# Idle matmuls in the boot, and one decay level to a phase instead of two, in an fp32 linear-attention and feed-forward kernel

## The chip, the core and the metric

The kernel runs on one core of one Trainium2 chip. The metric is device time in microseconds (us), the median of three runs. A core has a matmul engine (TensorE, called PE in the profile, with its weight loads apart as PEld), two elementwise engines (VectorE, called DVE, and ScalarE, called ACT), GpSimd (POOL), and queues that start transfers (SP is one). Each works through its own instructions in order and waits for the others by semaphores. Matmul results land in PSUM, everything else lies in SBUF.

## What is computed

```python
# first: linear attention with a decaying state, 4 batches, 8 heads, 768 tokens, 48 channels
for t in range(S):
    kt, vt, rt, wt = (k[:, :, t], v[:, :, t], r[:, :, t], w[:, :, t])
    cur = np.einsum('bhd,bhe->bhde', u[None] * kt, vt)
    y[:, :, t] = np.einsum('bhd,bhde->bhe', rt, state + cur)
    state = wt[:, :, :, None] * state + np.einsum('bhd,bhe->bhde', kt, vt)
# then, with x = y as (3072 tokens, 384 channels): w_in is (384, 2048), w_out is (2048, 384)
h = x @ w_in
g = h - np.tanh(h)
out = g @ w_out
```

All of it is fp32. The kernel cuts the 768 tokens of a batch in two, which makes eight blocks of 384 tokens. Within a block, chunks of 64 tokens are worked out by matmuls: the scores between a token and the earlier ones of its chunk are found level by level (spans of m = 1, 2, 4, 8, 16, 32). At each level the keys (`kq`) and receptances (`rp`) are multiplied by the decays of their half spans ("decay"), after the level's matmuls ("gram") have read them, and the part of the scores that belongs to the level is kept.

## The kernel before

The first block's attention is a stage of its own, the boot. After that, the feed-forward part of one block (16 steps f of 128 hidden columns: three matmuls into `hp`, elementwise work, and three steps later three matmuls into `acc`) runs with the attention of the next block in its gaps. The score buffers, the gram and the decay:

```python
    def scratch(ps):
        return ps.tile([P, 2, BANK], F32, name="att", tag="att")     # two PSUM banks
...
        def gram(self, ps, lhs, rhs, p0, n, m, width):               # 12 small matmuls for each of n pairs
            ps_t = scratch(ps)
...
                            nc.tensor.matmul(dst, lhsT=lhs[rows, t0:t0 + L], rhs=src,
                                             start=True, stop=True)
            return used
...
        def decay(self, m, p0, n, which=("kq", "rp")):
...
                ins = nc.vector.tensor_tensor(out=part, in0=part, in1=by, op=ALU.mult)
            return ins

        def level(self, ps, m, p0, n, put_off=None):
            if m == L // 2:
                copies = self.last_level(ps, p0, n)
                if put_off is None:
                    copies()
                else:
                    put_off.append(copies)
                return self.decay(m, p0, n)
            gr = self.gram(ps, self.tiles["kq"], self.tiles["rp"], p0, n, m, L // 2)
            ins = self.decay(m, p0, n)
            self.keep(gr, m, p0, n)
            return ins
```

Two levels in one phase need a second copy of `kq` and `rp`, one before and one after the first level's decay. The half that the decay changes is written there by VectorE, the other half is copied by ScalarE:

```python
        def decay_apart(self, m, name):
...
            nc.vector.tensor_tensor(out=dst[:, :, half, :], in0=src[:, :, half, :], in1=by, op=ALU.mult)

        def copy_half(self, m, name):
...
            nc.scalar.copy(out=dst[:, :, half, :], in_=src[:, :, half, :])

        def two_levels(self, ps, m):
            for i, level in enumerate((m, 2 * m)):
                gr = self.gram(ps, self.pairs["kq"][i], self.pairs["rp"][i], 0, NPAIR, level, L // 2)
                self.keep(gr, level, 0, NPAIR)
...
            self.decay(2 * m, 0, NPAIR)
```

The plan tells at which step f which phase of the next block's attention is put. Block 0 (i == 0) has one level to a phase, the others two:

```python
        names = ("level 1", 2, 4, 8, 16, 32, "turn", "update", "result 1")
        if i == 0:
            steps = (0, 2, 4, 5, 6, 7, 9, 10, 12)
...
        else:
            names = ("level 1", (2, 4), (8, 16), 32, "turn", "update", "result 1")
            steps = (2, 5, 8, 9, 10, 11, 13)
            before = {0: ("totals 1",), 1: ("totals 2", "kq"), 2: ("rp",), 3: (("by", 2, "kq"),),
                      4: (("by", 2, "rp"),), 6: (("by", 8, "kq"), ("by", 8, "rp"))}
            front = {4: (("copy", 2, "kq"),), 5: (("copy", 2, "rp"),), 7: (("copy", 8, "kq"), ("copy", 8, "rp"))}
```

The boot works in two halves of the head pairs, so that one half's gram stands beside the other's decay. The last level's copies (`last`) are put off behind the transposes (`turn`):

```python
        for m in (2, 4, 8, 16, 32):
            for p0 in HALVES:
                if (m, p0) != (2, h1):
                    ins = blk.level(ps, m, p0, UP, last)
                if p0 == h2 or m == 32:
                    blk.totals(m, p0, UP)
...
        for p0 in HALVES:
            blk.turn(ps, p0)
        for copies in last:
            copies()
        later.mix(0, NPAIR, ("kmix",))
        for p0 in HALVES:
            blk.update(ps, p0)
...
    with tc.tile_pool(name="ps_boot", bufs=4, space=PSUM) as ps_boot:
        xT = blocks[0].begin()
        boot(ps_boot, blocks[0], blocks[1])
```

Of the kernel before, what the change touches and what calls it, by code (L numbers as in the profile page):

```python
# [37 lines left out]
F32 = mybir.dt.float32  # L38
# [46 lines left out]
def kernel(  # L85
# [26 lines left out]
    u_sb = const.tile([P, NPAIR], F32, name="u_sb", tag="u_sb")  # L112
    nc.scalar.dma_start(out=u_sb, in_=uT)

    warm = const.tile([P, 1], F32, name="warm", tag="warm")
    nc.scalar.activation(out=warm, in_=shift[:, 0:1], func=AF.Copy)

# [65 lines left out]
    class Block:  # L183


        def __init__(self, b, q):
            self.b, self.q = b, q
            self.cols = slice(q * NB, (q + 1) * NB)
            self.tiles = {}
            self.tots = {}  # L190
            self.ks = {}
            self.pairs = {}

        def load(self, name, src, p0, n):
            if name not in self.tiles:
# [82 lines left out]
# [7 lines that stand above are left out]
                return self.decay(m, p0, n)  # L285
            gr = self.gram(ps, self.tiles["kq"], self.tiles["rp"], p0, n, m, L // 2)
            ins = self.decay(m, p0, n)
            self.keep(gr, m, p0, n)
            return ins

        def keep(self, gr, m, p0, n):
            nb = L // (2 * m)
            if 2 * m % 32 == 0:

                for par in range(2):
                    for b in range(nb):
                        s0, t0 = 64 * par + 2 * m * b, 2 * m * b + m
                        dst = A[s0:s0 + m, :, p0:p0 + n].rearrange("s h p c t -> s h (p c) t")
                        src = gr[s0:s0 + m].rearrange("s h (n b m) -> s h n b m", b=nb, m=m)
                        nc.scalar.copy(out=dst[:, :, :, t0:t0 + m], in_=src[:, :, :, b, :])  # L300
                return
            for h in range(2):
                dst = A[:, h, p0:p0 + n].rearrange("s p c (b two m) -> s (p c) b two m",
                                                   two=2, m=m)[:, :, :, 1, :]
                src = gr[:, h].rearrange("s (n b m) -> s n b m", b=nb, m=m)
                mask = masks[m].bitcast(U8).unsqueeze(1).to_broadcast([P, n * NCP, nb, m])
                nc.vector.copy_predicated(out=dst, mask=mask, data=src)  # L307


        def decay_apart(self, m, name):  # L310

            if name not in self.pairs:
                self.pairs[name] = [self.tiles[name], conv.tile([P, NPAIR * NB], F32, name=name + "_2",
                                                               tag="raw")]
            src, dst = self.pairs[name]
            tot, half = self.tots[m, 0], 0 if name == "kq" else 1
            t2 = tot.rearrange("d (n two) -> d n two", two=2)
            src, dst = (t.rearrange("d (n two m) -> d n two m", two=2, m=m) for t in (src, dst))
            by = t2[:, :, 1 - half].unsqueeze(2).to_broadcast([P, NPAIR * NB // (2 * m), m])
            nc.vector.tensor_tensor(out=dst[:, :, half, :], in0=src[:, :, half, :], in1=by, op=ALU.mult)  # L320

        def copy_half(self, m, name):
            half = 1 if name == "kq" else 0
            src, dst = (t.rearrange("d (n two m) -> d n two m", two=2, m=m) for t in self.pairs[name])
            nc.scalar.copy(out=dst[:, :, half, :], in_=src[:, :, half, :])

        def two_levels(self, ps, m):
            for i, level in enumerate((m, 2 * m)):
                gr = self.gram(ps, self.pairs["kq"][i], self.pairs["rp"][i], 0, NPAIR, level, L // 2)
                self.keep(gr, level, 0, NPAIR)  # L330
            for name, (src, dst) in self.pairs.items():
                self.tiles[name] = dst
                self.pairs[name] = [dst, src]
            self.decay(2 * m, 0, NPAIR)

        def last_level(self, ps, p0, n):

# [139 lines left out]
        def phase(self, ps, name):  # L477
            if name == "level 1":
                for p0 in HALVES:
                    self.level_1(ps, p0)()  # L480
            elif name == "turn":
                for p0 in HALVES:
                    self.turn(ps, p0)
            elif name == "update":
                for p0 in HALVES:
                    self.update(ps, p0)
            elif name in ((2, 4), (8, 16)):
                self.two_levels(ps, name[0])
            elif name == "result 1":
                self.parts = self.result_1(ps, list(range(NPAIR)))  # L490
            elif name == "result 2":
                self.result_2(*self.parts)
                self.fill_holes([nc.sync])
            else:
                self.level(ps, name, 0, NPAIR)


        def prepare(self, name):
# [5 lines left out]
            elif name == "totals 1":  # L504
                for m in (1, 2):
                    self.totals(m, 0, NPAIR)
            elif name == "totals 2":
                for m in (4, 8, 16, 32):
                    self.totals(m, 0, NPAIR)
            elif name in ("kq", "rp"):  # L510
                self.decay(1, 0, NPAIR, (name,))
            else:
                what, m, which = name
                (self.copy_half if what == "copy" else self.decay_apart)(m, which)


    def first(xT, f, ps):
# [49 lines left out]
    def plan(i):  # L567

        names = ("level 1", 2, 4, 8, 16, 32, "turn", "update", "result 1")
        if i == 0:  # L570

            steps = (0, 2, 4, 5, 6, 7, 9, 10, 12)
            before, front, urgent = {}, {}, (4, 5, 6)
            converted = (3, 4, 5, 5, 7, 9, 9, 10, 11, 13)
            loads = {f: "weights" for f in (0, 1, 2, 3, 4, 6, 7, 8, 9, 10)}
            loads.update({5: "v", 11: "rmix", 12: "kmix", 13: "wt", 14: "kq", 15: "rp"})
        else:
            names = ("level 1", (2, 4), (8, 16), 32, "turn", "update", "result 1")
            steps = (2, 5, 8, 9, 10, 11, 13)
            before = {0: ("totals 1",), 1: ("totals 2", "kq"), 2: ("rp",), 3: (("by", 2, "kq"),),  # L580
                      4: (("by", 2, "rp"),), 6: (("by", 8, "kq"), ("by", 8, "rp"))}
            front = {4: (("copy", 2, "kq"),), 5: (("copy", 2, "rp"),), 7: (("copy", 8, "kq"), ("copy", 8, "rp"))}
            converted, urgent = (), ()
            loads = {2: "v", 5: "rmix", 7: "kmix", 9: "wt", 11: "kq", 14: "rp"}
        return dict(zip(steps, names)), before, front, converted, loads, urgent

    blocks = [Block(b, q) for b in range(B) for q in range(NQ)]
    ctx.enter_context(tc.manual_schedule(engines={PE, SP, DVE, ACT}))
# [12 lines left out]
        tc.add_manual_dep(dma.ins, ins.ins.name, mybir.DependencyInfo(  # L601
            mybir.DependencyClass.Sync, mybir.DependencyReason.DATA))

    def boot(ps, blk, later):

        h1, h2 = HALVES
        for p0 in HALVES:
            for name, src in (("kq", kT), ("rp", rT), ("wt", wT)):
                blk.load(name, src, p0, UP)
# [5 lines left out]
            more_weights(nc.sync)  # L615
        blk.mix(h1, UP, copy=nc.vector.tensor_copy)
        masked = blk.level_1(ps, h1)
        blk.decay(1, h1, UP)
        blk.totals(1, h1, UP)
        blk.mix(h2, UP, copy=nc.scalar.copy)  # L620
        masked()
        blk.level(ps, 2, h1, UP)
        masked = blk.level_1(ps, h2)
        blk.decay(1, h2, UP)
        blk.totals(1, h2, UP)
        for m in (2, 4, 8, 16):
# [5 lines left out]
        for m in (2, 4, 8, 16, 32):  # L632
            for p0 in HALVES:
                if (m, p0) != (2, h1):
                    ins = blk.level(ps, m, p0, UP, last)
                if p0 == h2 or m == 32:
                    blk.totals(m, p0, UP)
            if m in background:
# [34 lines left out]
            converted()  # L673
            later.prepare(name)

    with tc.tile_pool(name="ps_boot", bufs=4, space=PSUM) as ps_boot:
        xT = blocks[0].begin()
        boot(ps_boot, blocks[0], blocks[1])
    ps_d = ctx.enter_context(tc.tile_pool(name="ps_d", bufs=1, space=PSUM))
    ps_a = ctx.enter_context(tc.tile_pool(name="ps_a", bufs=2, space=PSUM))  # L680
    waiting, rest, extra = [], [], []
# [11 lines left out]
    for i, blk in enumerate(blocks):  # L693
# [2 lines left out]
        after = blocks[i + 2] if i + 2 < len(blocks) else None  # L696
        if later:
            xT = later.begin()
        phases, before, front, converted, loads, urgent = plan(i)
        second = Second(blk.b * S + blk.q * NB, ps_d)  # L700
        for f in range(NF):
            if later:
                for name in front.get(f, ()):
                    later.prepare(name)
            g, next_rest, made = first(here, f, ps_d)
            waiting.append((second, f, g))
            if f not in urgent:
# [1 line left out]
            if later:  # L709
                for name in before.get(f, ()):  # L710
                    later.prepare(name)
                if f in phases:
                    later.phase(ps_a, phases[f])
            if after and f >= NF - 2:
                after.prepare("kmix" if f == NF - 2 else "rmix")
            if f in urgent:

                finish(rest, extra)
# [69 lines left out]
```

## Time and profile before

| what | value |
|---|---|
| device time, three runs | 678.99, 681.27, 680.66 us; median 680.66 |
| span of the profiled run (678.99 us) | 677.2 us, mean granted TensorE clock 0.977 |
| VectorE busy, share of the span | 546.6 us, 81% |
| ScalarE busy, share of the span | 508.3 us, 75% |
| acc and hp matmuls (L558, L520) | 768 records each, 280.1 and 274.3 us busy |
| grams of the levels 2 to 16 (L243, 48x32) | 3072 records, 56.6 us busy |
| half copies of two-level phases (L325, ScalarE) | 24, 10.4 us (rp) and 10.3 us (kq) busy |
| decays apart (L320, VectorE) | 24, 11.4 us (rp) and 11.4 us (kq) busy |

How to read it: the page of the profile gives each engine's busy time and the chain of work that ended last, followed back from the end. A line of a group names the source line (L243), the engine, the operation, the tiles as out<-in, shape and count (x192). A number in brackets with an arrow, such as [0.82 <-issue], is idle time of that engine just before and what ended it; "issue" means that the engine waited for nothing that the profile shows. In order of time, the first number is the start and the second the length, in us. A line by stages has the stretch, its length, then busy time and count of TensorE matmuls, of weight loads, VectorE, ScalarE and GpSimd, then granted TensorE clock, busy share of the transfer engines and GB/s. Matmuls overlap and their ends are modelled, so that starts are the better measure of pace.

### The profile page before, as it was taken

The page shows a single profiled execution, that of the slowest core. Times are in us where ns is not written, and L with a number is a line of the kernel's source. Part 1 is how long each engine was busy: PE and PEld are TensorE (multiplying, and loading weights), DVE is VectorE, ACT ScalarE, POOL GpSimd, SP SyncE. Part 2 cuts the span into 40 slices and gives each one's busy share as a digit, 9 for nine tenths or more (in the row PEclk, how much of TensorE's full clock was granted, in tenths as well). Part 3 has the DMA queues.
Part 4 walks back from the last instruction along what each step waited for, and adds up shares of the span by engine and source line. Part 5 has one row for each costly group of instructions (what it writes and reads, how often), then busy time and mean ns, then how long its engine had stood idle before and what let it go on. Part 6 is the DMA issues. An engine that isn't in the chain of part 4 may idle for free.

```text
span 677.2 us, 20000 instructions
## 1 busy us (share of the span) xinstructions
PE 648.8 (96%) x8480; PEld 414.6 (61%) x8480; DVE 546.6 (81%) x1101; ACT 508.3 (75%) x992; POOL 4.9 (1%) x19
## 2 busy tenths in 40 slices
PE   5879999999999999999999999999999999999998
PEld 4745556666666656666665656656666666665554
DVE  7779999997769968699887976779867998756764
ACT  4779898876767767687868857678676868778785
POOL 2000000000000000000000000000000000000000
PEclk9969999998999989999999988999999999999999
DMA  8656343431303113221311221113211210000000
GB/s 316 231 181 207 130 142 107 150 106 48 92 13 110 56 49 95 57 71 49 95 48 56 79 89 48 48 57 100 67 51 51 84 40 2 2 11 36 0 0 36
DMA packets 30842, 54.38 MB, mean 80 GB/s; under 512 B 2336, under 2 KB 28704, under 8 KB 30752
## 3 DMA queue, kind: packets, MB, share of 16 engines
q1 hardware_dynamic: 30336, 52.80, 24.2%
q8 instruction: 67, 1.10, 0.7%
q10 hardware_dynamic: 352, 0.25, 0.1%
q14 instruction: 23, 0.19, 0.1%
q0 software_dynamic: 64, 0.05, 0.0%
HBM read 47.19 MB, written 4.72 MB: 77 GB/s over the span
## 4 chain that ended last, share of the span: by engine, by line
PE 87%; DVE 5%; ACT 3%; issue 2%; DMA 1%; PEld 0%; PEldq 0%; SPq 0%; DVEq 0%
PE acc L558 36%; PE hp L520 36%; PE att L243 8%; PE att L437 2%; PE att L419 2%; PE att L373 2%; PE att L391 1%; PE att L350 1%; DVE rp L275 1%; DVE w_sb L175 1%; DMA wt<-in_wT 1%; DVE hs L537 1%; DVE kq L275 1%; DVE scores L307 1%; ACT scores L361 1%
## 5 line engine op out<-in xcount | busy, mean ns | idle before, releaser
L558 PE MATMUL acc<-w_sb,gT 128*128 128x384 f32 x768 | 280.1, 503 | 0.8
L520 PE MATMUL hp<-xT,w_sb 128*128 128x384 f32 x768 | 274.3, 494 | 4.8 <-ACT xT L465 2.1
L520 PEld LDWEIGHTS hp<-xT,w_sb 128*128 128x128 f32 x768 | 146.9, 193 | 110.5 <-issue 6.1
L558 PEld LDWEIGHTS acc<-w_sb,gT 128*128 128x128 f32 x768 | 144.7, 194 | 94.9 <-issue 6.4
L527 ACT ACTIVATE h<-hp 128x384 f32<-128x384 f32 x128 | 62.7, 490 | 116.6 <-PE hp L520 115.6
L542 DVE TENSOR_TENSOR th<-h,th 128x384 f32<-128x384 f32 x128 | 71.0, 555 | 43.9 <-ACT th L531 43.9
L537 DVE SCALAR_TENSOR_TENSOR hs<-h,s 128x384 f32<-128x384 f32 x128 | 70.8, 553 | 22.7 <-ACT s L528 22.7
L545 DVE COPY_PREDICATED gT<-big,th 128x384 f32<-128x384 int32 x128 | 76.3, 596 | 12.4
L529 ACT ACTIVATE qa<-s,shift 128x384 f32<-128x384 f32 x128 | 78.8, 615 | 4.2
L537 DVE SCALAR_TENSOR_TENSOR gT<-qb,hs 128x384 f32<-128x384 f32 x128 | 71.4, 558 | 10.1
L532 ACT ACTIVATE big<-s,shift 128x384 f32<-128x384 f32 x128 | 76.8, 600 | 0.0
L530 ACT ACTIVATE qb<-s,shift 128x384 f32<-128x384 f32 x128 | 76.7, 600 | 0.0
L537 DVE SCALAR_TENSOR_TENSOR hs<-qa,hs 128x384 f32<-128x384 f32 x128 | 70.6, 552 | 0.0
L528 ACT ACTIVATE s<-h 128x384 f32<-128x384 f32 x128 | 67.0, 523 | 4.0
L531 ACT ACTIVATE th<-h 128x384 f32<-128x384 f32 x128 | 64.9, 507 | 0.0
L243 PEld LDWEIGHTS att<-rp,kq 48*64 48x64 f32 x3072 | 53.4, 146 | 18.3 <-issue 11.1
L243 PE MATMUL att<-rp,kq 48*64 48x32 f32 x3072 | 56.6, 229 | 8.0 <-issue 6.0
L275 DVE TENSOR_TENSOR kq<-kq,tot 128x768 f32<-128x768 f32 (+1 forms) x33 | 27.4, 830 | 15.1 <-PE att L350 7.9
L402 DVE SCALAR_TENSOR_TENSOR states<-states,tot,att 128x48 f32<-128x48 f32 x176 | 31.5, 258 | 8.7 <-PE att L391 8.7
L307 DVE COPY_PREDICATED scores<-mask_all,att 128x384 f32<-128x384 uint8 (+1 forms) x54 | 31.4, 663 | 2.3 <-PE att L243 1.7
L275 DVE TENSOR_TENSOR rp<-rp,tot 128x768 f32<-128x768 f32 (+1 forms) x33 | 27.3, 828 | 0.0
L243 PE MATMUL att<-rmix,kmix 48*64 48x64 f32 x768 | 14.5, 232 | 6.7 <-ACT rmix L223 6.7
(58 smaller groups left out, 379.4 us busy)
## 6 DMA issues: line engine op xcount, KB each, us to landing
raw<-in_weights SPq DMA_DIRECT2D x16, 768.0 KB, 4.7
rmix<-in_rT SPq DMA_DIRECT2D x7, 768.0 KB, 4.7
kmix<-in_kT SPq DMA_DIRECT2D x7, 768.0 KB, 4.6
wt<-in_wT SPq DMA_DIRECT2D x7, 768.0 KB, 4.6
kq<-in_kT SPq DMA_DIRECT2D x7, 768.0 KB, 5.4
rp<-in_rT SPq DMA_DIRECT2D x7, 768.0 KB, 4.7
v_sb<-in_v SPq DMA_DIRECT2D x8, 576.0 KB, 4.6
out_y<-o SPq DMA_DIRECT2D x23, 192.0 KB, 1.9
```

Source lines behind the costliest of these rows:

```text
L243: nc.tensor.matmul(dst, lhsT=lhs[rows, t0:t0 + L], rhs=src, start=True, stop=True)
L275: ins = nc.vector.tensor_tensor(out=part, in0=part, in1=by, op=ALU.mult)
L520: nc.tensor.matmul(hp, lhsT=w_in_sb[:, f, kc, :], rhs=xT[:, kc, :], start=(kc == KC - 1), stop=(kc == 0))
L528: nc.scalar.activation(out=s, in_=h, func=AF.Square)
L529: nc.scalar.activation(out=qa, in_=s, func=AF.Square, bias=shift[:, 0:1])
L530: nc.scalar.activation(out=qb, in_=s, func=AF.Square, bias=shift[:, 1:2])
L531: nc.scalar.activation(out=th, in_=h, func=AF.Tanh)
L532: nc.scalar.activation(out=big, in_=s, func=AF.Relu, bias=shift[:, 2:3])
L537: return lambda: nc.vector.scalar_tensor_tensor(out=out, in0=in0, scalar=scalar, in1=in1, op0=op0, op1=ALU.mult)
L542: lambda: nc.vector.tensor_tensor(out=th, in0=h, in1=th, op=ALU.subtract),
L545: lambda: nc.vector.copy_predicated(out=g, mask=big.bitcast(I32), data=th)], made
L558: nc.tensor.matmul(acc, lhsT=g[:, j * P:(j + 1) * P], rhs=w_out_sb[:, f, :], start=(f == 0), stop=(f == NF - 1))
```

## The change

The change has two parts.

In the boot, TensorE gets 16 matmuls whose results nobody reads: 128x128 by 128x384 in fp32, on a tile of ones, into a PSUM bank of their own. They are meant for TensorE's waits, to keep the engine busy there. Four stand at the start and one behind each half level. The bank they need is taken from the boot's score buffers, three of two banks each instead of four.

In blocks 1 to 6, levels 2, 4, 8 and 16 get a phase each, as in block 0, instead of two for each pair of levels. The second tiles, the decays that write there and the half copies go; the ordinary decay in place is used for all levels. The multiplications of `kmix` and `rmix` by u move from the last two steps of a block to the first two of the next, and the other preparations move later by two steps.

```diff
+    idle_in = const.tile([P, NB], F32, name="idle_in", tag="idle_in")
+    nc.vector.memset(idle_in, 1.0)
     warm = const.tile([P, 1], F32, name="warm", tag="warm")
...
-        def decay_apart(self, m, name):
...
-        def copy_half(self, m, name):
...
-        def two_levels(self, ps, m):
...
         else:
-            names = ("level 1", (2, 4), (8, 16), 32, "turn", "update", "result 1")
-            steps = (2, 5, 8, 9, 10, 11, 13)
-            before = {0: ("totals 1",), 1: ("totals 2", "kq"), 2: ("rp",), 3: (("by", 2, "kq"),),
-                      4: (("by", 2, "rp"),), 6: (("by", 8, "kq"), ("by", 8, "rp"))}
-            front = {4: (("copy", 2, "kq"),), 5: (("copy", 2, "rp"),), 7: (("copy", 8, "kq"), ("copy", 8, "rp"))}
-            converted, urgent = (), ()
+            steps = (4, 5, 6, 7, 8, 9, 10, 11, 13)
+            before = {0: ("kmix",), 1: ("rmix",), 2: ("totals 1",), 3: ("totals 2", "kq"), 4: ("rp",)}
+            behind, converted, urgent = {}, (), ()
...
-    def boot(ps, blk, later):
+    def boot(ps, ps_idle, blk, later):
 
         h1, h2 = HALVES
+        spare = ps_idle.tile([P, NB], F32, name="spare", tag="spare")
+
+        def keep_busy(n):
+
+            for _ in range(n):
+                nc.tensor.matmul(spare, lhsT=idle_in[:, 0:P], rhs=idle_in, start=True, stop=True)
+
+        keep_busy(4)
...
         masked = blk.level_1(ps, h1)
+        keep_busy(1)
...
         blk.level(ps, 2, h1, UP)
+        keep_busy(1)
         masked = blk.level_1(ps, h2)
+        keep_busy(1)
...
                 if (m, p0) != (2, h1):
                     ins = blk.level(ps, m, p0, UP, last)
+                    keep_busy(1)
...
-    with tc.tile_pool(name="ps_boot", bufs=4, space=PSUM) as ps_boot:
+    with tc.tile_pool(name="ps_boot", bufs=3, space=PSUM) as ps_boot, \
+            tc.tile_pool(name="ps_idle", bufs=1, space=PSUM) as ps_idle:
         xT = blocks[0].begin()
-        boot(ps_boot, blocks[0], blocks[1])
+        boot(ps_boot, ps_idle, blocks[0], blocks[1])
...
-            if after and f >= NF - 2:
-                after.prepare("kmix" if f == NF - 2 else "rmix")
```

## The prediction

> **What bounds the kernel now.** I read the page's busy row and chain first, then TensorE's instructions in order of time, then what TensorE waited for, stage by stage, then VectorE's order of time in one block and in the boot.
>
> ```profile
> PE 648.8 (96%) x8480; PEld 414.6 (61%) x8480; DVE 546.6 (81%) x1101; ACT 508.3 (75%) x992; POOL 4.9 (1%) x19
> ...
> PE 87%; DVE 5%; ACT 3%; issue 2%; DMA 1%; PEld 0%; PEldq 0%; SPq 0%; DVEq 0%
> ```
>
> TensorE sets the time, and of its 677.2 us 28.4 are idle. What PE's busy time hides is its clock. The output copies (L563) close every block and mark its length: they start at 135.61, 217.55, 298.67, 376.43, 460.14, 541.15 and 618.89 us. The periods are 81.94, 81.12, 77.76, 83.71, 81.01 and 77.74. Two of six are alike to 0.02 us; the other four are longer by 4.2, 3.4, 5.95 and 3.25, **16.8 us in all**. In the order of time, a two-level phase in an undisturbed block (first two lines) and one in a long block:
>
> ```profile
> 323.64 3.00 PE L243 MATMUL att<-rp,kq 48*64 48x32 f32 x192
> 326.57 2.20 PE L558 MATMUL acc<-w_sb,gT 128*128 128x384 f32 x6
> ...
> 145.85 2.76 PE L243 MATMUL att<-rp,kq 48*64 48x32 f32 x174
> 149.43 0.74 PE L243 MATMUL att<-rp,kq 48*64 48x32 f32 x18 [0.82 <-issue]
> 150.11 4.21 PE L558 MATMUL acc<-w_sb,gT 128*128 128x384 f32 x6
> 154.10 2.99 PE L520 MATMUL hp<-xT,w_sb 128*128 128x384 f32 x6
> ```
>
> A phase is 192 matmul records (every fp32 matmul leaves two, each with its weight load). In the second TensorE stops for 0.8 us in mid-phase, with "issue" as the only cause, and the dense matmuls after it take twice as long. The stages around it:
>
> ```profile
> 143.80:149.10 5.30, 4.81 (x181) 3.60 (x180) 5.09 (x9) 5.21 (x10) 0.00 (x0) 1.00 0.26 64
> 149.10:155.90 6.80, 6.47 (x27) 3.80 (x27) 5.92 (x11) 0.00 (x0) 0.00 (x0) 0.50 0.19 70
> 155.90:159.30 3.40, 3.40 (x12) 2.01 (x11) 2.02 (x3) 2.10 (x5) 0.00 (x0) 1.00 0.00 0
> ```
>
> The third number from the end is the granted clock: 0.50 for 6.8 us. Over the blocks, what TensorE waited for shows the same event five times, and little else:
>
> ```profile
> PE att L243 <- issue: 5.6, 5, 1.4
> PE hp L520 <- DVE w_sb L175: 1.6, 4, 0.6
> ```
>
> All five lie in the twelve two-level phases (stops of 0.82, 1.38, 1.21, 0.93, 1.27 us); about thirty single bursts of the same density but half the length show none. Each time a 16 KB packet of the instruction queue starts 1.0 to 1.7 us into the phase (at 147.22 in the case shown), TensorE runs dry shortly after and goes on 2.2 to 2.9 us after the packet's start.
>
> **The boot** (0 to 42.90, the first hp) is the other stretch with a wrong clock:
>
> ```profile
> 15.48 1.51 PE L243 MATMUL att<-rp,kq 48*64 48x32 f32 x48 [0.33 <-DVE rp L275]
> 17.52 6.02 PE L243 MATMUL att<-rp,kq 48*64 48x32 f32 x187 [0.53 <-DVE rp L275]
> ...
> 42.90 4.05 PE L520 MATMUL hp<-xT,w_sb 128*128 128x384 f32 x6 [2.07 <-ACT xT L465]
> ```
>
> 48 records in 1.51 us are 31 ns each; in the blocks 192 take 3.00, 15.6 ns. So the boot's levels run at half clock, although the page prints 9 there (the trace's clock records begin only at 29.6 us). But VectorE is as full there: in 12 to 24.3 us it is busy 11.42 of 12.30 us.
>
> **What the Trainium skill says.** "TensorE: Matmul & The Clock Gate", Part 1 (The HAM clock gate): the clock is halved by default, a busy window of about 3.4 us releases it, an idle one takes it back. The trace agrees: cold spells of 3.4 and 6.8 us, and full rate 3.8 us after the first hp. Part 4 (PE-mode transpose) of that page says transposes don't count as busy; the first clock record (1.00 at 29.6 us) follows 2.8 us of fp32 transposes, so here they seem to. "Runtime: NRT & Kernel Launch", Instruction fetch mechanics: instructions come in blocks of 256 and crossing is "mostly hidden". A two-level phase has 384 TensorE instructions and must cross one; the five stops show it is not always hidden. "PSUM — Partial Sum Buffer", Specifications: eight banks of 512 fp32 values. A score buffer here is two, so four fill PSUM and the idle bank costs the fourth; no trace line bears on that.
>
> **The change part by part.**
>
> 1. *Phases split (blocks 1 to 6).* Same matmuls, same decays on VectorE (two for each level either way; out of place or in place both about 0.95 us). ScalarE loses 24 half copies of 0.86 us, 20.7 us, but no TensorE wait in an undisturbed block names it: worth nothing directly. Each phase is now 96 matmul records, 192 instructions. Block 0 already runs so: its level bursts last 1.53 us start to start (53.77 to 55.30) against 2.93/2 = 1.465, and the dense group before and the one after each cost about 0.1 more than 1.935. Two more bursts in a block: 2 x (0.065 + 0.2) = 0.53, **+3.2 us** in six blocks.
>
> 2. *The stops.* After a fetch starts, TensorE has work for at least 1.0 us (mostly 1.2 to 1.65) at burst rate. A single level lasts 1.5, so only a fetch that falls on its first few tenths can bite. Block 0 has four such bursts without a stop and without a cold spell. Most of the 16.8 us goes. I keep 1.5 back for a few stops of 0.6 us: **-15.3 us**.
>
> 3. *Does a new wait appear?* A level now needs the decay of the level before one step earlier. A step on TensorE is 1.94 (hp) + 1.53 + 1.94 (acc) + 0.1 = 5.5 us. VectorE: five products 2.7 (302.61 to 306.22 less one 0.86 decay, start to start), decays 1.73, masked copies 1.7 (m = 2) or 0.93: 6.1, 5.4, 5.4. Laid out from the end of one hp, with the gram at 5.6 to 7.1: previous copies done by 5.1, products to 7.8, decays to 9.55; the next gram wants them at 11.1. Slack 1.5 us, though one step is over budget by 0.6. Block 0 waited for a decay once, 0.23 us, with converts on top. **0**. The u products move from steps 14 and 15 to steps 0 and 1, where VectorE has 3.6 us of work in 3.87: **0**.
>
> 4. *Idle matmuls.* 4 + 3 + 9 = 16, each two records of 0.323 us warm: 0.645, 10.3 us in all (twice that cold). The first four start behind the memset at about 1.5 us and, cold, end at 1.5 + 8 x 0.65 = 6.7; the first gram started at 5.92. They are over 3.4 us of solid work, so I expect the clock up before they end: delay 0.3. Then a half level is 0.75 (24 matmuls warm) + 0.645 + 0.2 of switching = 1.6 us on TensorE, against VectorE's 1.55 (0.47 + 0.47 for decays, 0.53 to 0.62 for copies, totals between) and today's 1.5. So levels hardly get faster. What goes is VectorE's waits near the end (0.93 at 24.46, some 0.6 at the last level): -1.5, and half the transposes' 2.8 us: -1.4.
>
> 5. *Three buffers.* The last level's two stay occupied until its put-off copies, which stand behind both transposes' copies on ScalarE. The second transposes and the first update wait for one buffer: one copy, 0.8, plus 0.6 of handing over: **+1.4**. After that nothing is kept busy; TensorE idles, 24 state updates on VectorE (30.28 to 34.57) and ScalarE copies set the pace, and the clock falls as today. The 4.05 us first hp stays.
> Sum for the boot: 0.3 - 1.5 - 1.4 + 1.4 = **-1.2 us**.
>
> Total: 3.2 - 15.3 - 1.2 = -13.3 us against the profiled run, 678.99: 665.7. The median before is 680.66, and the undisturbed level the blocks fall to is common to all runs, so a run with more stops gains more; the boot's guess has an edge downwards as well (an issue stop of 2.25 us at 33 us shifts by 64 instructions). I say **665.0 us**.
>
> **Rivals.**
> *A: the cold boot stays cold.* If four idle matmuls don't release the clock, each half level is 1.5 + 1.3 = 2.8 us, 9 x 1.25 = 11 us lost: about 676. For it: the levels alone never warmed it. Against: five to six microseconds of dense matmuls, while the first hp (42.90) reached full rate in 3.8. One in twelve.
> *B: the decay chain becomes the wait.* If VectorE lags by 1 us more than laid out, every level waits about 1 us: 24 x 1 = 24 us, and 689. For it: VectorE is over budget in one step of each block. Against: block 0, with more work, waited 0.23. One in thirty.
> *C: stops have nothing to do with phase length.* Then stops and cold spells return in other bursts and only the boot counts: about 680. Against: five of twelve long phases, none of the short. One in ten.
> *D: no stop at all and a fully warm boot tail* (another 2 us at the first hp): about 660.
>
> **Range and chances.** 2% faster is below 667.05. Main line 662 to 668 by the boot's and the remaining stops' uncertainty; A and C carry the upper end. 80%: 659.5 to 671.5. Faster 0.73, same 0.25, slower 0.02.
>
> **What would show it.** Periods between output copies of 78.0 to 78.6 in blocks 1 to 6; no 0.50 clock after 50 us; "att <- issue" under 2 us; boot grams at 15 to 16 ns a record and the first hp at 41 to 43. Wrong if TensorE waits for "DVE rp" or "kq" in the blocks by more than 3 us, if half clock reappears in the blocks, or if the first hp comes after 45.

## The result, and the profile after

The changed kernel takes 670.13 us (median of four runs, 669.34 to 673.36), the kernel before 680.96 us beside it (678.99 to 681.42). The ratio is 0.9855, with a 95% interval of 0.9817 to 0.9893: 1.45% faster, 10.8 us. The range of the prediction holds it, but the time lies 5.1 us above the 665.0 named, and "faster by over 2%", to which 0.73 was given, did not come about; a change of under 2%, given 0.25, did.

The span of the profiled run went from 677.2 to 668.7 us, by 8.5. Cut at the first `hp` and at the first output copy of each block, it splits so:

| stretch | before | after | difference |
|---|---|---|---|
| boot, up to the first hp | 42.90 | 48.01 | **+5.1** |
| first hp to the first output copies | 92.71 | 91.89 | -0.8 |
| six block periods | 483.28 | 470.47 | **-12.8** |
| last of these copies to the end | 58.3 | 58.3 | 0 |

So the blocks gave all that was hoped for, and the boot, which was to give 1.2 us, took 5.1.

The busy row and the chain of the page after:

```profile
PE 650.9 (97%) x8512; PEld 409.3 (61%) x8512; DVE 545.8 (82%) x1102; ACT 490.0 (73%) x968; POOL 4.6 (1%) x19
...
PE 90%; DVE 4%; ACT 3%; issue 2%; PEld 1%; PEldq 0%; DVEq 0%
```

TensorE is busy for 2.1 us more than before in a span that is 8.5 us shorter; ScalarE, without its half copies, is busy for 18.3 us less. "issue" still holds 2% of the chain. Two levels of a block, in TensorE's order of time (start, length):

```profile
150.13 1.60 PE L244 MATMUL att<-rp,kq 48*64 48x32 f32 x96
151.66 2.20 PE L524 MATMUL acc<-w_sb,gT 128*128 128x384 f32 x6
153.70 2.10 PE L486 MATMUL hp<-xT,w_sb 128*128 128x384 f32 x6
155.73 1.60 PE L244 MATMUL att<-rp,kq 48*64 48x32 f32 x96
```

A level is now 96 records in 1.53 us from start to start, with dense matmuls between one level and the next. The periods between output copies are 78.41 us five times and 78.42 once, where before they were 77.74 to 83.71. What TensorE waited for from 48 us to the end has no line with "issue":

```profile
PE hp L486 <- ACT xT L436: 2.1, 1, 2.1
PE hp L486 <- DVE w_sb L177: 1.2, 3, 0.6
PE hp L486 <- ACT h L493: 0.6, 1, 0.6
```

The stages (the third number from the end is the granted clock): full clock to 34.7 us, half clock for 17 us around the first hp, full clock in the blocks.

```profile
7.30:34.70 27.40, 22.49 (x656) 14.82 (x650) 19.96 (x50) 14.00 (x29) 0.00 (x0) 1.00 0.72 251
34.70:51.70 17.00, 12.02 (x260) 8.98 (x251) 13.96 (x40) 11.18 (x24) 1.11 (x2) 0.50 0.40 135
51.70:300.00 248.30, 245.63 (x3200) 153.66 (x3200) 216.05 (x426) 196.89 (x384) 0.00 (x0) 1.00 0.33 103
```

So the idle matmuls did release the clock, and TensorE kept it through all nine half levels. The boot is longer all the same. Its order of time after, from the start to the first hp:

```profile
1.49 5.49 PE L575 MATMUL spare<-idle_in 128*128 128x384 f32 x8 [1.49 <-DVE idle_in L116]
...
20.05 0.32 PE L244 MATMUL att<-rp,kq 48*64 48x32 f32 x8 [1.10 <-issue]
...
24.48 0.90 PE L244 MATMUL att<-rp,kq 48*64 48x32 f32 x48
25.32 0.91 PE L575 MATMUL spare<-idle_in 128*128 128x384 f32 x2
...
29.57 0.25 PE L321 MATMUL att<-rp,kq 48*32 48x32 f32 x4 [1.42 <-issue]
...
32.21 0.88 PE L344 MATMUL att<-ident,kq 128*128 128x128 f32 x6 [0.89 <-ACT ks L346]
33.97 0.99 PE L362 MATMUL att<-v_sb,ks 64*64 64x48 f32 x48 [0.89 <-ACT ks L346]
...
38.71 1.30 PE L408 MATMUL att<-scores,v_sb 64*48 64x64 f32 x36 [1.61 <-issue]
...
48.01 2.29 PE L486 MATMUL hp<-xT,w_sb 128*128 128x384 f32 x3 [2.07 <-ACT xT L436]
```

The reader is to see four things: a half level of 0.84 us with 0.84 us of idle matmuls behind it (24.48 to 25.32, and 25.32 to 26.16); stops of 1.10, 1.42 and 1.61 us in which TensorE waits for nothing that is shown; the two waits of 0.89 us for a score buffer; and the first hp at 48 us, waiting for ScalarE's `xT` at the end of all this.

### The profile page after: what moved, and what is told of

Same layout as the page of the kernel before. It is cut to its first block, busy times and chain, and to the rows that moved or that the text cites. A ratio compares the mean times of both kernels' runs of the same rounds, so it can differ in the third digit from the quotient of the medians.

```text
span 668.7 us, 20035 instructions
## 1 busy us (share of the span) xinstructions
PE 650.9 (97%) x8512; PEld 409.3 (61%) x8512; DVE 545.8 (82%) x1102; ACT 490.0 (73%) x968; POOL 4.6 (1%) x19
## 4 chain that ended last, share of the span: by engine, by line
PE 90%; DVE 4%; ACT 3%; issue 2%; PEld 1%; PEldq 0%; DVEq 0%
PE hp L486 36%; PE acc L524 36%; PE att L244 9%; PE spare L575 2%; PE att L390 2%; PE att L408 2%; PE att L344 1%; PE att L362 1%; PE att L321 1%; DVE w_sb L177 1%; DVE hs L503 1%; ACT h L493 0%; DVE gT L511 0%; DVE rp L276 0%; ACT w_sb L172 0%
## 5 line engine op out<-in xcount | busy, mean ns | idle before, releaser
L524 PE MATMUL acc<-w_sb,gT 128*128 128x384 f32 x768 | 273.7, 493 | 0.8
L486 PEld LDWEIGHTS hp<-xT,w_sb 128*128 128x128 f32 x768 | 145.2, 191 | 107.6 <-ACT xT L436 2.3
L524 PEld LDWEIGHTS acc<-w_sb,gT 128*128 128x128 f32 x768 | 140.5, 190 | 89.9 <-ACT o L529 2.3
L511 DVE COPY_PREDICATED gT<-big,th 128x384 f32<-128x384 int32 x128 | 76.1, 595 | 12.8 <-ACT h L493 0.5
L244 PEld LDWEIGHTS att<-rp,kq 48*64 48x64 f32 x3072 | 48.4, 135 | 21.6 <-issue 16.7
L244 PE MATMUL att<-rp,kq 48*64 48x32 f32 x3072 | 52.6, 220 | 1.7 <-issue 1.6
L276 DVE TENSOR_TENSOR kq<-kq,tot 128x768 f32<-128x768 f32 (+1 forms) x45 | 38.7, 860 | 5.1 <-PE att L321 3.7
L276 DVE TENSOR_TENSOR rp<-rp,tot 128x768 f32<-128x768 f32 (+1 forms) x45 | 38.9, 864 | 0.0
L172 ACT ACTIVATE w_sb<-raw 128x768 f32<-128x768 f32 x16 | 14.6, 914 | 6.0 <-DMA raw<-in_weights 5.8
```

The lines of the kernel that those rows point to most:

```text
L244: nc.tensor.matmul(dst, lhsT=lhs[rows, t0:t0 + L], rhs=src, start=True, stop=True)
L486: nc.tensor.matmul(hp, lhsT=w_in_sb[:, f, kc, :], rhs=xT[:, kc, :], start=(kc == KC - 1), stop=(kc == 0))
L511: lambda: nc.vector.copy_predicated(out=g, mask=big.bitcast(I32), data=th)], made
L524: nc.tensor.matmul(acc, lhsT=g[:, j * P:(j + 1) * P], rhs=w_out_sb[:, f, :], start=(f == 0), stop=(f == NF - 1))
```

## The experiments

Where a run was made beside its own runs of the kernel before, the ratio is to those; two executions, of 687.22 and 956.04 us, that were slow as a whole are left out of the times. The boots compare best stage by stage (us; "turn" is the first transpose, "update" the first `att<-v_sb,ks`, "scores" the first `att<-scores,v_sb`, "states" the first `att<-rp,states` of the boot; "stops" is the sum of TensorE's waits named "issue" up to the first hp):

| kernel | first gram | grams to turn | turn to update | to scores | to states | to first hp | first hp at | stops |
|---|---|---|---|---|---|---|---|---|
| before | 5.92 | 20.39 | 2.75 | 2.13 | 4.48 | 7.24 | 42.90 | 2.68 |
| after | 6.90 | 23.60 | 3.47 | 2.48 | 3.67 | 7.88 | 48.01 | 4.62 |
| changed boot, long phases | 6.91 | 24.12 | 4.27 | 2.60 | 2.08 | 7.73 | 47.70 | 3.12 |
| phases split, old boot | 6.05 | 21.10 | 2.65 | 2.13 | 4.57 | 7.88 | 44.37 | 3.04 |
| three buffers, no idle matmuls | 5.82 | 20.98 | 4.86 | 2.59 | 2.47 | 6.75 | 43.47 | 0.71 |
| idle matmuls, four buffers | 5.97 | 22.18 | 1.71 | 1.86 | 1.96 | 7.24 | 40.93 | 0.73 |
| the same again | 6.27 | 23.31 | 2.69 | 2.13 | 1.96 | 6.75 | 43.12 | 2.65 |
| the same, narrow idle matmuls | 6.91 | 23.71 | 2.70 | 2.12 | 1.96 | 6.75 | 44.15 | 0.99 |
| phases split, 32 tiny matmuls ahead | 5.70 | 21.87 | 2.75 | 2.25 | 1.84 | 6.73 | 41.12 | 1.62 |

**One part alone: the phases.** The changed kernel with the boot of the kernel before (four buffers, no idle matmuls).

```diff
-        keep_busy(4)
-                    keep_busy(1)        # and the three others
-    ... tc.tile_pool(name="ps_boot", bufs=3, space=PSUM) as ps_boot, \
-            tc.tile_pool(name="ps_idle", bufs=1, space=PSUM) as ps_idle:
+    with tc.tile_pool(name="ps_boot", bufs=4, space=PSUM) as ps_boot:
```

> The boot as before (four buffers, no idle matmuls), blocks 1 to 6 with one level to a phase. If the two parts of the change add up: first hp at 42.9 us (before 42.90, after 48.01), periods between output copies 78.4 us as in the changed kernel, no stop in the blocks, no half clock after 50 us; 665 us in all (663.5 to 667). If instead the blocks needed the boot's new clock or its shifted instructions to run clean, stops come back and it is 668 to 680.

Measured: 667.03 us (666.22 to 668.06) against 679.05, ratio 0.9836 [0.9772, 0.9900]. All periods are 78.41 or 78.42, and TensorE's waits after 45 us name no "issue". The first hp came at 44.37, 1.5 us later than expected, and the stop in the boot's tail is there, 2.33 us:

```profile
33.22 0.54 PE L406 MATMUL att<-scores,v_sb 64*48 64x64 f32 x21 [0.75 <-ACT scores L330]
36.09 0.31 PE L406 MATMUL att<-scores,v_sb 64*48 64x64 f32 x3 [2.33 <-issue]
```

The split phases alone do the whole of the gain. All their times lie below all of the whole change's (669.34 and more), and their first hp comes 3.6 us sooner; the intervals of the two ratios overlap.

**The other part alone: the boot.** The kernel before, two levels to a phase, with the changed boot.

```diff
+        keep_busy(4)
...
+                    keep_busy(1)        # and the three others
...
-    with tc.tile_pool(name="ps_boot", bufs=4, space=PSUM) as ps_boot:
+    ... bufs=3 ..., ps_idle bufs=1
```

> The changed boot alone, blocks 1 to 6 with two levels to a phase as before. Theory F (TensorE runs dry at a border between instruction blocks of 256, and only where a burst has run without a break for over some 258 instructions before that border): the 16 idle matmuls shift all later instructions by 66, so of the twelve two-level phases the 1st, 2nd, 5th, 8th and 11th stop (borders 284, 338, 366, 317, 345 instructions into the phase), the 7th (263) perhaps; the 4th and 10th, which stopped before, don't (235, 246). Time 684 to 690. Theory T (stops come from the transfers that run beside the phase): the same phases as before, 1, 4, 7, 8, 10. Theory C (chance): no pattern. All: first hp near 48.0.

Measured: 677.78 us (673.94 to 683.56, 19 runs) against 679.05, ratio 1.0007 [0.9978, 1.0036]. The first hp came at 47.70, 4.8 us late, and still the time did not move, where 684 to 690 was expected: the periods are 80.56, 77.86, 82.02, 79.31, 77.76 and 82.00, which is 13.0 us above six times 77.75, where the kernel before has 16.8. The boot's change has altered the blocks behind it, without altering one instruction in them. Before, stops were in the two-level phases 1, 4, 7, 8 and 10 (counted from 1 to 12); here they are in 2, 5, 8 and 11, four of the five phases that were named; phase 1, with a border 284 instructions in, did not stop. The one in phase 2:

```profile
164.35 2.65 PE L245 MATMUL att<-rp,kq 48*64 48x32 f32 x168
167.98 0.80 PE L245 MATMUL att<-rp,kq 48*64 48x32 f32 x24 [0.98 <-issue]
```

So the place of a stop follows from what was issued on TensorE earlier. The numbers come from counting TensorE's instructions in a trace (matmuls, weight loads, waits and drains, in their order). The stops of before stand at instruction 960, 1473, 4544, 7105, 10945, 11457 and 13504, those of over 0.3 us in this run, but for one of 0.31 at 322, at 704, 1217, 1472, 5056, 8896, 11457 and 15297, the three of over 1 us in the boot after at 704, 1217 and 1472: **all at 192 or 193 beyond a multiple of 256.** Call such a place a border. This is the theory of borders ("Theory F" above; it had put the bound at some 258 instructions), and the next runs were made to break it.

**Shift the borders, leave the phases long.** The kernel before, with 32 tiny matmuls (48x64 by 48x32, result unread) at the start of the boot: 128 instructions, half the distance between two borders.

```diff
+        spare = scratch(ps)
+        for n in range(32):
+            at = 64 * (n % 2)
+            nc.tensor.matmul(spare[0:64, n % 2, 0:32], lhsT=idle_in[at:at + D, 0:64],
+                             rhs=idle_in[at:at + D, 0:32], start=True, stop=True)
```

> The kernel before, with 32 small matmuls (48x64 on a tile of ones, 32 columns, unread) at its start, where TensorE waits for its first data anyway: 128 more instructions and one wait, nothing else. Theory F (borders of 256 instructions; a two-level phase stops when a border lies more than some 290 instructions into it): the phases that stop are now the 3rd, 5th, 6th and 12th (borders 374, 303, 357, 336), the 2nd and 11th (275, 282) at most briefly; the 1st, 4th, 7th, 8th and 10th, which stopped before, run through. Theory T (transfers beside the phase): 1, 4, 7, 8, 10 as before. First hp within 1.5 us of before's 42.9; 674 to 681 us.

Measured: 669.52 us in one run, with the first hp at 40.48; both are lower than expected. Stops are in phases 3, 5, 6 and 12, and one that was not in the list, right behind phase 9, ahead of the first `acc`. The one in phase 3:

```profile
220.20 2.98 PE L245 MATMUL att<-rp,kq 48*64 48x32 f32 x186
223.99 0.31 PE L245 MATMUL att<-rp,kq 48*64 48x32 f32 x6 [0.80 <-issue]
224.23 3.85 PE L560 MATMUL acc<-w_sb,gT 128*128 128x384 f32 x6
```

With the three kernels there are 36 two-level phases. This is how many of a phase's 384 instructions lie ahead of its last border, with * where TensorE stopped:

```text
phase          1    2    3    4    5    6    7    8    9    10   11   12
before         350* 148  247  301* 176  230  329* 383* 258  312* 155  209
changed boot   284  338* 181  235  366* 164  263  317* 192  246  345* 143
32 tiny ahead  221  275  374* 172  303* 357* 200  254  385* 183  282  336*
```

Up to 284 none stops, from 301 on every one does. The expected list of phases held but for the 385, which is one instruction past the phase's end: the burst had by then run the whole 384 without a pause.

**Put every border where it is harmless.** The kernel before with its long phases, the 32 tiny matmuls at the start, and 39, 21 and 21 more in the "turn" phases of three blocks, counted so that no border has more than 275 of a phase's instructions ahead of it.

```diff
+            for n in range(pads):
+                at = 64 * (n % 2)
+                nc.tensor.matmul(tp[at:at + 64, n % 2, NB:NB + 32], lhsT=idle_in[at:at + D, 0:64],
+                                 rhs=idle_in[at:at + D, 0:32], start=True, stop=True)
...
+                pads = {2: 39, 4: 21, 6: 21}.get(blocks.index(self), 0)
```

> The kernel before, two levels to a phase, with nothing changed but the places of the borders: 32 small unread matmuls at the start and 39, 21 and 21 in the transposes' phase of three blocks, laid out by the borders' arithmetic so that in none of the twelve phases a border lies more than 275 instructions in. Theory F: no stop in any phase, no half clock after 50 us, periods 77.7 to 79 us (the added matmuls are 0.6 to 1.2 us in three blocks), first hp near 40.5, 660 to 663 us, as fast as one level to a phase or faster. If phase length itself makes stops or cold spells: three to five of them again, 667 us or more.

Measured: 665.81 us (665.47 to 666.90, six runs) against 679.82, ratio 0.9810 [0.9773, 0.9847]. This is 2.8 us above the 660 to 663 expected. All twelve phases run through. TensorE's waits from 45 us on, and one phase:

```profile
PE hp L527 <- DVE w_sb L177: 1.6, 4, 0.6
PE hp L527 <- ACT h L534: 0.8, 1, 0.8
PE hp L527 <- ACT big L539: 0.2, 1, 0.2
```

```profile
238.52 3.00 PE L245 MATMUL att<-rp,kq 48*64 48x32 f32 x192
241.45 2.20 PE L565 MATMUL acc<-w_sb,gT 128*128 128x384 f32 x6
```

The periods are 77.75 three times and 80.36, 79.30 and 79.30 in the blocks with pads, which cost 2.6, 1.55 and 1.55 us (expected: 0.6 to 1.2). Adding 113 useless matmuls to the kernel before makes it 1.9% faster, without splitting anything; in the profiled runs 11.1 us of it lie in the six periods. That is the theory's strongest test: a long phase alone makes no stop, a border late in it does.

**Which half of the boot's change costs.** Two kernels with all split phases: one with three buffers and no idle matmuls, one with the idle matmuls and four buffers (they write into a score buffer, as no bank is left).

```diff
-        keep_busy(4)                   # three buffers, no idle matmuls
-                    keep_busy(1)
```

> The changed kernel without its idle matmuls, still with three score buffers in the boot. If the idle matmuls themselves lengthened the boot: first hp at 43.0 to 44.3 us, only the hand-over of buffers left (0.7 to 1.4 us over 42.9). If the missing fourth buffer did: 46.5 to 48.

```diff
-        spare = ps_idle.tile([P, NB], F32, name="spare", tag="spare")     # four buffers
+            spare = scratch(ps)[:, 0, 0:NB]
...
-        tc.tile_pool(name="ps_boot", bufs=3, ...), tc.tile_pool(name="ps_idle", bufs=1, ...)
+        tc.tile_pool(name="ps_boot", bufs=4, ...)
```

> The changed kernel with four score buffers; the idle matmuls write into a score buffer that nobody reads. If the idle matmuls lengthened the boot: first hp at 46.5 to 47.6 us. If the missing fourth buffer did: 42.5 to 44.

Measured: three buffers 667.02 us in one run, first hp 43.47, of which turn to update took 4.86 (2.1 more than before); but the tail's stop was gone, and that paid most of it back. Four buffers with idle matmuls: 663.31 us in one run, first hp 40.93, sooner than either case expected. The same kernel in four more runs:

> The changed kernel with four score buffers and its idle matmuls in a score buffer, timed: its one time was 663.31 against 667.03 with the boot as before. If that holds: 662 to 665 us, first hp at 40.5 to 42. If the one run was luck with the phase of the clock's window: 665 to 668.

663.72 us (662.21 to 665.43), ratio 0.9793 [0.9750, 0.9836], first hp 43.12. That the same kernel's boot ended once at 40.93 and once at 43.12 shows how far the lengths of stops scatter: they sum to 0.73 us in the one and 2.65 in the other, which leaves 40.2 and 40.5. Neither half alone is worth 5 us. In the first of the two traces the longest stop near the end of the levels is 0.56 us (1.42 in the changed kernel), and the twelve transposes run in one piece, 1.71 us to the update, where the changed kernel waits 0.89 twice.

**Does the warm clock pay for the idle matmuls?** Three runs. First, idle matmuls behind the half levels of 128 columns, not 384.

```diff
-        def keep_busy(n):
+        def keep_busy(n, width=P):
...
+                nc.tensor.matmul(spare, lhsT=idle_in[:, 0:P], rhs=idle_in[:, 0:width], start=True, stop=True)
```

> As the kernel with four buffers, but the idle matmuls behind the half levels are 128 columns wide instead of 384 (the four at the start stay). If TensorE's own time sets the pace of the levels there (0.84 + 0.84 us a half level): about 0.42 less for each of 9 half levels, turn at 26 to 26.7 instead of 28.2 us, first hp at 39 to 39.8, 661 to 662.5 us, as long as the clock stays up. If a narrow matmul is too little to hold the clock: half levels of 1.5 + 0.5 us, turn at 28 or later and 664 or more.

666.52 us (666.25 to 667.03), ratio 0.9832, first hp 44.15. The clock fell at 14.31 and stayed down in the levels; a half level shows it in its 1.44 us, with 0.72 for the idle ones:

```profile
14.71 1.28 PE L244 MATMUL att<-rp,kq 48*64 48x32 f32 x35 [0.74 <-issue]
...
16.64 1.51 PE L244 MATMUL att<-rp,kq 48*64 48x32 f32 x48
18.08 0.79 PE L575 MATMUL att<-idle_in 128*128 128x128 f32 x2
```

Second and third, no idle matmuls at all, four buffers, split phases, only the borders moved by 16 or by 32 tiny matmuls at the start.

```diff
+        for n in range(16):            # 32 in the other
+            nc.tensor.matmul(spare[0:64, n % 2, 0:32], lhsT=idle_in[at:at + D, 0:64],
+                             rhs=idle_in[at:at + D, 0:32], start=True, stop=True)
```

> One level to a phase, the boot as before with four buffers, and 16 small unread matmuls at the start: 64 instructions more, as many as the change's idle matmuls have, but too small to raise the clock. If the gain of four buffers with idle matmuls (first hp 40.93) is that TensorE's stop of 2.3 us ahead of the first result moved away: no stop over 1 us between 28 and 38 us, first hp at 41 to 42.3. If the gain is the clock: stop or not, first hp at 42.7 to 44.5.

> One level to a phase, the boot as before with four buffers, and 32 small unread matmuls at its start, which shift the borders by 128 instructions. In the kernel before the same 32 brought the first hp from 42.9 to 40.5 us. If that was the stop of 2.2 us in the boot's tail: first hp at 40 to 41.5 here too, no stop over 1 us between 30 and 37 us, 661.5 to 664 us. If it was chance: first hp at 42.5 to 44.5 and 665 to 667.

With 16: 664.68 us in one run, first hp 41.83; the tail's stop is gone, one of 1.96 us has come at 26 us. With 32: 663.65 us (663.32 to 664.67) against 675.8, ratio 0.9822 [0.9771, 0.9873], first hp 41.12. In its tail the matmuls that stood still for 2.33 us with the split phases alone stop for 0.34 at most:

```profile
32.28 0.49 PE L362 MATMUL att<-v_sb,ks 64*64 64x48 f32 x19 [0.34 <-issue]
...
33.73 0.55 PE L408 MATMUL att<-scores,v_sb 64*48 64x64 f32 x24 [0.57 <-ACT scores L332]
```

Both boots are at half clock up to the transposes, and both end as early as the warm one with four buffers. So the idle matmuls, with the warm clock that they bring to the levels, are worth nothing here. The gain of the shifted boot over the split phases alone (44.37 to 41.12) came with nothing changed but 128 instructions ahead: the stops named "issue" fell from 3.04 to 1.62 us, and the way from the states to the first hp, where none is named, is shorter by 1.15.

**Move the borders in the changed kernel.** The changed kernel with the 32 tiny matmuls ahead of its idle ones.

```diff
+        for n in range(32):
+            at = 64 * (n % 2)
+            nc.tensor.matmul(spare[at:at + 64, 0:32], lhsT=idle_in[at:at + D, 0:64],
+                             rhs=idle_in[at:at + D, 0:32], start=True, stop=True)
         keep_busy(4)
```

> The changed kernel with 32 small unread matmuls ahead of its idle ones, which shift its borders by 128 instructions and delay the first gram by about 1 us. The changed boot's stops were 0.49, 1.10, 1.42 and 1.61 us, and it took 41.1 us from the first gram to the first hp. If the stops' places made the loss: 37.5 to 39.5 us from first gram to first hp, stops under 2 us in all. If idle matmuls and buffers alone made it: 40.5 to 41.5.

One run: 669.84 us. The first gram came at 10.43, 3.5 us later (the tiny ones run at half clock, 3.6 us of them), and the first hp at 46.54, so the stretch between them shrank from 41.10 to 36.10. TensorE's waits up to the first hp have no "issue" among them; the two hand-overs of 0.89 remain, to the hundredth. The 5 us are an upper bound for the stops: the later start also lets loads land and VectorE get ahead, and a wait of 1.04 us put down to VectorE falls two instructions behind a border and ends 1.5 us after the end of a 16 KB packet, as the stops do (see below), so it may be a stop under another name.

**A warm clock at the first hp.** The split, shifted kernel with two idle matmuls right ahead of the first hp.

```diff
         ins = blk.result_2(*blk.result_1(ps, [h2, h2 + 1]), True)
+        spare = scratch(ps)[:, 0, 0:NB]
+        for _ in range(2):
+            nc.tensor.matmul(spare, lhsT=idle_in[:, 0:P], rhs=idle_in, start=True, stop=True)
```

> The same, and two idle matmuls (128x384, 2.6 us at half clock) in the one wait where dense matmuls follow at half clock: ahead of the first hp, while TensorE waits 2.1 to 2.9 us for the copies into xT. If the clock rises sooner by their length: first six hp records in 2.6 to 3.6 us instead of 4.1 to 4.2, 0.7 to 1.5 us faster than without. If the window happens to fall otherwise or they delay hp: within 0.5 us of it.

A miss: 664.69 us (663.99 to 665.12) against 663.65 without.

```profile
41.58 2.20 PE L486 MATMUL hp<-xT,w_sb 128*128 128x384 f32 x6
43.71 1.63 PE L244 MATMUL att<-rmix,kmix 48*64 48x64 f32 x96
46.86 3.86 PE L486 MATMUL hp<-xT,w_sb 128*128 128x384 f32 x6 [1.52 <-ACT h L493]
```

The first hp is done in 2.20 us, not 4, and the second then waits 1.52 us for ScalarE, and is cold itself. It starts at 46.86; without the idle matmuls at 46.51. The warm first hp gains nothing, as ScalarE paces the start of the feed-forward part.

## Why the prediction was right and where it failed

**Phases split, +3.2: right.** 78.41 against 77.75 in an undisturbed block is 0.66 a block (0.53 predicted), 4.0 us.

**The stops, -15.3: right, and the reserve of 1.5 was not needed.** All 16.8 us went. -16.8 + 4.0 = -12.8, which is what the six periods show. The working ("a fetch that falls on its first few tenths can bite") had the right event and the wrong variable. The packet's start is a consequence; what decides is how much of a burst lies ahead of a border. In the blocks of before, the 16 KB packet starts 0.43 to 1.05 us after TensorE has passed a border (the five cases: 146.53 to 147.22, 242.86 to 243.91, 387.21 to 387.64, 405.55 to 406.24, 485.54 to 486.42), and TensorE goes on 2.9 to 3.45 us after the border. A burst issues 256 instructions in 1.95 us (384 in 2.93), so TensorE reaches the next border first. With one level to a phase the burst is over after 192, and the dense matmuls, 12 instructions in 1.94 us each, give the packet time. On this point the page "Runtime: NRT & Kernel Launch" of the Trainium skill, section Instruction fetch mechanics, has blocks of 256 and a crossing that is "mostly hidden": the distance of 256 agrees with every stop, and in the blocks it is hidden unless a dense burst of some 290 instructions runs up to the border. That the packet of one border is what TensorE misses at the next shows in the times of all fourteen traces: they hold one 16 KB packet for each border, in the same order; in 925 pairs TensorE never passes a border sooner than 0.97 us after the end of the packet that belongs to the one before, and the 41 stops of over 0.3 us at a border all end 1.1 to 1.6 us after it. No run changed the packets themselves.

**New waits, 0: right.** No line of the blocks names a decay. From the first hp to the first output copies 0.8 us went, which was not predicted.

**Rivals.** A, the boot stays cold, fell: full clock from 7.37 us. The boot grew in another way. B fell: all six periods are 78.41 or 78.42. C fell: the shorter bursts of the blocks show no stop. D expected a warm tail to give 2 us at the first hp; the last experiment shows that it gives none.

**The boot, -1.2: the step that failed; it measured +5.1.** By its own terms:

- *Start, "delay 0.3"*: 6.90 against 5.92, +1.0. The eight records stayed cold to their end (the clock came at 7.37) and ended at 6.98, not 6.7, with the first gram behind them in TensorE's order. In the three traces with four buffers it came at 4.97, 4.94 and 7.48, and the first gram at 5.97, 6.27 and 6.91: this term varies from run to run.
- *"VectorE's waits near the end: -1.5"*: the levels took 23.60 us, 3.2 more. The stops in them grew from 0.44 to 3.01 (0.49, 1.10 and 1.42), and 0.6 is left for the idle matmuls' own time. The size per half level was right: 1.68 us against the 1.6 of the working and VectorE's 1.55. But the step took 0.05 us above VectorE as nothing, and did not let TensorE's stops add to it. Stops are paid where VectorE sets the pace, too: without idle matmuls the levels take 20.39 us with 0.44 of stops, 21.87 with 1.28 and 22.44 with 2.22 (before, and the split phases with 32 and with 16 tiny matmuls).
- *Transposes, -1.4*: -1.05. *Three buffers, +1.4*: two hand-overs of 0.89, +1.8. Both mechanisms right, and their sum from turn to update is +0.7, where 0 was predicted.
- *Stops left out.* The sum had no term for them in the boot; "an issue stop of 2.25 us at 33 us shifts by 64 instructions" was named as an edge downwards. It shifted, and turned into 1.10, 1.42 and 1.61, with a 0.49 that stands at no border: 4.62 us of stops in place of 2.68, +1.9.

Start 1.0, stops 1.9, levels without stops 0.6, turn to update 0.7 make 4.3 of the 5.1 (before rounding); update, scores and the end account for the rest, 0.8. The largest single term is the one left out, but 3.2 us of the 5.1 are no stops: less its stops, the boot ends at 43.4, against 40.2 before. The same idle matmuls with four buffers end at 40.2 and 40.5 less their stops, so by this estimate, which takes each stop as paid in full, three buffers beside idle matmuls cost about 3 us, where the prediction had 1.4; without idle matmuls they cost 1.4 (42.8 against 41.3). The changed boot with long phases has 1.5 us less of stops and its first hp only 0.3 sooner, so the split is that of one trace: in this other boot the clock fell at 31.57, and turn to update took 4.27. Why the stops of the changed boot are longer than those of the same idle matmuls with four buffers isn't settled. In the changed boot the packet behind the border passed at 29.57 starts at 36.37, 6.8 us later, while the weights are coming in (the transfer engines are busy for 0.75 of that stretch, and without a break from 33 us on); in the five stopped phases of before it is under 1.1. That the transfers hold it up was not tried.

That the time still lies in the range is owed to its width and to the blocks. "Wrong if the first hp comes after 45" was the mark that was passed; the rest of what was to show it (periods of 78.0 to 78.6, no half clock in the blocks) came about; the boot's grams took 17.5 ns a record (0.84 us for 48), not 15 to 16.

The two best kernels, four buffers with idle matmuls (663.7 us) and split phases with 32 tiny matmuls (663.65), were run on chips of their own, where the kernel before had medians of 677.3 and 675.8; their runs end at 665.4 and 664.7, those of the changed kernel begin at 669.3.

## What to carry to other kernels

When TensorE stops for "issue" in a dense burst, number its instructions before blaming the clock or the load: if the stops share a remainder of 256, shorten the burst or move the border with a few cheap matmuls, and expect any change of the instruction count to move every stop behind it. So judge a change of a kernel's start by the start alone, and the blocks behind by their undisturbed period. Matmuls put into waits to keep the clock up take the time that they warm: in these levels, which VectorE paced, they gained nothing.

## What the runs showed of the hardware

- Stops of over 0.5 us named "issue" stand at 192 or 193 mod 256 of TensorE's instructions in all traces read here, boot and blocks. In the blocks they last 0.8 to 1.4 us, and a block with one of them is longer by 1.6 to 4.3 us, with the half clock that mostly follows; in the boot they last up to 2.33.
- 32 tiny matmuls at the start, 128 instructions, take about 8 us off the kernel before (669.52 in one run against a median of 677.3).
- The clock falls without an idle stretch of 3.4 us: it was lost in or within 1.8 us of 11 of the 14 stops in the blocks (all five of the kernel before, three of four with the changed boot, three of five with 32 tiny matmuls), where an idle stretch is never over 1.4 us. On the Trainium skill's page "TensorE: Matmul & The Clock Gate", Part 1 (The HAM clock gate), it is idle that takes the clock back. Here TensorE was busy for 2.95 of the 3.41 us ahead of the fall at 149.07, with grams alone (175 records); in the changed boot it kept the clock from 27.85 to 31.26 with 1.99 us busy, mostly idle matmuls and transposes (37 records). That small matmuls count for less than they fill is a reading of this; no run varies it alone.
- Idle matmuls of 384 columns every 1.68 us or so held the clock to the end of the levels in four of five traces; in the fifth it fell at 28.83, behind a stop of 1.38. With 128 columns it fell at 14.31, behind 3.41 us with 1.97 busy, in which one wait of 1.10 us and the first half of one of 0.74 lie.
